# Sums and scales of four expert weights with priority, and their halves and the last transposes in another order, in a fused attention and mixture-of-experts kernel

## The chip, the cores and the metric

The kernel runs on one core of a Trainium2 chip. The metric is the device time of one launch in microseconds. The median of three runs of the kernel before is 670.71 us (669.89 to 672.58).

## The reference

Three layers follow one another over 1152 tokens with 512 features: attention that keeps the 32 largest scores of a row, a gated feed-forward layer behind an RMS norm, and a routed layer in which each token goes to one of eight experts.

```python
scores = scale * q @ k.T                                  # 2 x 8 heads, 576 x 576, head_dim 64
kth = 32nd largest of a row
attn = softmax(where(scores >= kth, scores, -1e9)) @ v
x = attn                                                  # 1152 x 512
xn = x / sqrt(mean(x * x) + 1e-6) * rms_g
x = (silu(xn @ w_gate) * (xn @ w_val)) @ w_out            # d_ff 1536
logits = x @ w_gate2                                      # 8 experts
e, p = argmax(logits), softmax(logits)[argmax]
out = p * (relu(x @ w1[e]) @ w2[e])                       # d_ff 1024; the first `capacity` = 288 tokens of an expert
```

## The kernel before, in words

The tokens are worked in nine tiles of 128 (NT = 9, tile 8 is the last). A hand-written order of slots (`at`, `advance`) sets when each part is traced: `topk`, `weights` and `values` (attention), `norm`, `moe1` (the gated layer) and `dispatch` (routing, and the scatter of a token's row into a table `disp` in DRAM, one region for each expert). Each part is a generator, and slots of several tiles interleave. What is traced gets a priority by its place in the program; `tc.high_priority(offset)` raises it. A list scheduler then fixes the order of every engine's queue from priorities and its own estimate of times; on the chip each queue runs in that order. `tc.issue_after(x)` keeps the instructions of a block that run on x's engine behind x in that queue; it does nothing to the other engines' instructions of the block. `after(t, name)` is such a tie to an instruction that was noted in `behind`.

Matrix products are done with numbers split into two fp16 halves, three matmuls for a product (high x high, high x low, low x high).

`norm` (L435) ends in four transposes into PSUM and `halves` (L469): ScalarE writes the high half of the transposed tile (L470), VectorE the low half (L471). `moe1` (L479) takes three groups of 512 hidden features; for each it makes a gate and a value product of 12 matmuls (L500), a tanh on ScalarE (L507), and two VectorE steps (L508, L511) that give the hidden tile h. `turned` (L483) transposes h in four matmuls (L486) and calls `halves` on the result, hT. The second product sums over 12 steps f of three matmuls (L525); steps 0 to 3 read hT of group 0, 4 to 7 that of group 1, 8 to 11 that of group 2. The result yx is copied by ScalarE (L531).

`dispatch` (L536) transposes yx (L540), multiplies by the router's matrix (L554), takes the logits (L557), makes the token's expert (L577 to L591), counts its place in the expert by two or three small matmuls (L593 to L595, L602), and gets the row number `slot` (L615). GpSimd then scatters the row (L617). For the last tile the gather of expert 0's first 128 rows (call k = "a", L612, issued by ScalarE's queue) starts as soon as the router's input is there; rows that the last tile adds to expert 0 are gathered later, by an indirect DMA of GpSimd (`rest_gather`, L890, k = "b") and a transposing DMA of SP's queue (L894).

The experts' weights w1 and w2 are 16 matrices of 2 MB, taken in the order 0, 1, 2, 3, 4, 6, 5, 8, 7 and so on (number 2e is w1 of expert e, 2e + 1 is w2). Each is loaded by SP's queue (L775). `size` (L780) squares it on ScalarE, in four pieces of 1024 columns for the first four weights (L791), casts the sums on VectorE (L794), adds them over the partitions by one matmul for each piece against ones (L796), and makes a power of two from the sum in five small VectorE steps (L797 to L802, with L148 and L151), one more for w2 (L806). `convert` (L809) makes the two halves: for the first four weights two pieces of the high half on ScalarE (L816), two on VectorE (L818), and four pieces of the low half on VectorE (L821). Weights 0 and 1 are loaded into the places that later hold the halves of weights 2 and 3, and the buffer of weight 2 takes weight 4 once weight 2's halves are made.

Around the change, `whole` traces these calls after the token tiles: `size(0)`, `size(1)`, `convert(0)`, `size(2)`, `convert(1)`, `convert(2)` with its VectorE part behind the last `halves` of tile 8, `size(3)`; then, behind the last router product on TensorE, the up product of expert 0's first 128 rows (`up("a")`, L907), `convert(3)` with its VectorE part behind the last `halves` of tile 8, the gathers for experts 1 to 3, and the loop over the experts, in which `ready` sizes and converts the later weights. `up` copies a product's relu as two halves (L917 on ScalarE, L918 on VectorE), `down` scales with VectorE (L926), `send` transposes back, scales and scatters the rows to the output (L985).

Of the kernel before, what the change touches and what calls it, by code (L numbers as in the profile page):

```python
# [1 line left out]

# [17 lines left out]
P = 128  # L20
# [42 lines left out]
def whole(  # L63
# [371 lines left out]
    def norm(t, ew):  # L435
        rs = mx.tile([P, H], F32, name="rs", bufs=2)
        (nc.gpsimd if t < NT - 1 else nc.vector).tensor_scalar(rs, sums[t], EPSD, None, op0=OP.add)
        yield
        nc.vector.reciprocal(rs, rs)
        u, v = ("xu", "x") if t < NT - 1 else ("x", "xu")  # L440
        xu = mx.tile([P, KC, P], F32, name=u)
        nc.scalar.activation(xu, xps.pop(t), AF.Copy)
        yield
        bank = "px" if t < NT - 1 else "xps"
        xt = px.tile([P, KC, P], F32, name=bank)
        for c in range(KC):
            nc.tensor.transpose(xt[:, c, :], xu[:, c, :], ident)
        x = mx.tile([P, DM], F32, name=v)
        nc.scalar.activation(x, xt.rearrange("p c j -> p (c j)"), AF.Copy)
        yield  # L450
        x3 = x.rearrange("p (h d) -> p h d", h=H)
        ew.tensor_tensor(x3, x3, rs[:, :, None].to_broadcast([P, H, D]), op=OP.mult)
        sq = mx.tile([P, DM], F32, name=u)
        ss = mx.tile([P, 2], F32, name="ss", bufs=2)
        nc.scalar.activation(sq, x, AF.Square, accum_out=ss[:, 0:1])
        yield
        nc.gpsimd.tensor_scalar(ss[:, 1:2], ss[:, 0:1], XS ** -2 / DM, XS ** -2 * 1e-6, op0=OP.mult, op1=OP.add)
        nc.gpsimd.tensor_tensor(ss[:, 0:1], ss[:, 1:2], mhalf, op=OP.pow)
        yield
        nc.scalar.activation(sq, x, AF.Copy, scale=ss[:, 0:1])  # L460
        yield
        xnT[t] = mx.tile([P, 2 * KC, P], F16, name="xn")
        xn = px.tile([P, KC, P], F32, name=bank)
        for c in range(KC):
            nc.tensor.transpose(xn[:, c, :], sq[:, c * P:(c + 1) * P], ident)
        halves(xnT[t], xn)
        yield

    def halves(out, x):  # L469
        nc.scalar.activation(out[:, :KC], x, AF.Copy)  # L470
        return nc.vector.tensor_tensor(out[:, KC:], x, out[:, :KC], op=OP.subtract)  # L471

    yx, late, behind = {}, [], {}

    def after(t, engine):

        return tc.issue_after(behind[t, engine].ins)

    def moe1(t, ew):  # L479
        hT = [mx.tile([P, 2 * KC, P], F16, name="hT", bufs=3) for _ in range(3)]  # L480
        xn = xnT.pop(t)

        def turned(g, h):  # L483
            tp = pm.tile([P, 4, P], F32, name="pm")
            for i in range(4):
                nc.tensor.transpose(tp[:, i, :], h[:, i * P:(i + 1) * P], ident)  # L486
            behind[t, "dve"] = halves(hT[g], tp)

        h = None
        for g in range(3):  # L490
            th = mx.tile([P, DM], F32, name="th")
            if ew is nc.gpsimd:
                gs = mx.tile([P, DM], F32, name="gs")
            for w in range(2):
                b = 2 * g + w
                a = late[0].tile([P, DM], F32, name="late") if late and b % 3 else pm.tile([P, DM], F32, name="pm")
                for c in range(KC):
                    i = KC * b + c
                    for n, (x, lo) in enumerate(((0, 0), (0, 1), (KC, 0))):
                        nc.tensor.matmul(a, xn[:, x + c, :], half(i, lo), start=(c == 0 and n == 0), stop=(c == KC - 1 and n == 2))  # L500
                    if c == 1:
                        yield
                    if c == 0 and w == 0 and h is not None:
                        turned(g - 1, h)
                yield
                if w == 0 and ew is nc.vector:
                    nc.scalar.activation(th, a, AF.Tanh, scale=gdec[:, g:g + 1])  # L507
                    nc.vector.scalar_tensor_tensor(th, th, 1.0, a, op0=OP.add, op1=OP.mult)  # L508
                elif ew is nc.vector:
                    h = mx.tile([P, DM], F32, name="x" if t == NT - 1 and g == 1 else "gs")  # L510
                    nc.vector.scalar_tensor_tensor(h, a, vg[:, g:g + 1], th, op0=OP.mult, op1=OP.mult)  # L511
                elif w == 0:
                    nc.scalar.activation(th, a, AF.Tanh, scale=gdec[:, g:g + 1])
                    nc.scalar.activation(gs, a, AF.Copy, scale=gdec[:, g:g + 1])
                    ew.tensor_tensor(th, th, gs, op=OP.mult)
                    ew.tensor_tensor(th, th, gs, op=OP.add)
                else:
                    h = mx.tile([P, DM], F32, name="gs")
                    nc.scalar.activation(h, a, AF.Copy, scale=vdec[:, g:g + 1])
                    ew.tensor_tensor(h, th, h, op=OP.mult)  # L520
        yps = pm.tile([P, DM], F32, name="pm")
        for f in range(NF1):
            i = final(6, f)
            for n, (hi, lo) in enumerate(((0, 0), (0, 1), (1, 0))):
                nc.tensor.matmul(yps, hT[f // KC][:, KC * hi + f % KC, :], half(i, lo), start=(f == 0 and n == 0), stop=(f == NF1 - 1 and n == 2))  # L525
            if f == 3:
                turned(2, h)
            if f % 2 == 1:
                yield
        yx[t] = route.tile([P, DM], F32, name="yx")  # L530
        nc.scalar.activation(yx[t], yps, AF.Copy, scale=ydec)  # L531
        yield
# [3 lines left out]
    def dispatch(t):  # L536
# [75 lines left out]
                gather("a", 0, 0, WA, ew, nc.scalar)  # L612
                notes("a", 0, 0, WA, ew, nc.scalar)
        slot = route.tile([P, 1], I32, name="slot")
        ev.tensor_scalar(slot, pos[:, 0:1], pos[:, 1:2], pos[:, 2:3], op0=OP.add, op1=OP.add)  # L615
        nc.gpsimd.tensor_tensor(cum, cum, oh, op=OP.add)
        scat.append(nc.gpsimd.indirect_dma_start(  # L617
            out=disp, out_offset=bass.IndirectOffsetOnAxis(ap=slot[:, :1], axis=0),
# [161 lines left out]
    def size(j, n):  # L780
# [5 lines left out]
        for g in range(k):  # L786
            if exact:
                junk = mx.tile([P, DM], F32, name="th").bitcast(BF16)
            else:
                junk = ew.tile([P, BIG], BF16, name="junk")[:, :2 * BIG // k]  # L790
            nc.scalar.activation(junk, raw[:, g * 2 * BIG // k:(g + 1) * 2 * BIG // k], AF.Square, accum_out=sc[:, 9 + g:10 + g])  # L791
        t = sums_of[:, n % 8:n % 8 + 1]
        s16 = ew.tile([P, 4], BF16, name="s16", bufs=2)
        nc.vector.tensor_copy(s16[:, :k], sc[:, 9:9 + k])  # L794
# [9 lines left out]
            es[e] = sc  # L804
        else:
            nc.vector.tensor_tensor(es[e][:, 8:9], es[e][:, 4:5], sc[:, 4:5], op=OP.mult)  # L806
        sized[j] = sc

    def convert(j, n):  # L809

# [53 lines left out]
    px.release()  # L864
    pm.release()
    wts.release()
    size(0, 0)
    size(1, 1)
    convert(0, 0)
    size(2, 2)  # L870
    convert(1, 1)
    with after(NT - 1, "dve"):
        convert(2, 2)
    fetch_w()
# [115 lines left out]

    with after(NT - 1, "pe"):
        up("a", 0, WA)
    with after(NT - 1, "dve"):
        convert(3, 3)
    last = gather(1, 1, 0, W, eb, nc.sync)
    rest_gather()
# [116 lines left out]
```

## Time and profile before

| | |
|---|---|
| median of 3 runs | 670.71 us |
| the profiled execution | 669.08 us |
| its span, first to last instruction | 667.2 us |
| mean granted TensorE clock | 0.975 |
| TensorE (PE) busy | 585.2 us, 88% |
| TensorE weight load (PEld) busy | 410.9 us, 62% |
| VectorE (DVE) busy | 535.9 us, 80% |
| ScalarE (ACT) busy | 500.5 us, 75% |
| GpSimd (POOL) busy | 353.6 us, 53% |
| chain that ended last | PE 54%, DVE 17%, DMA 9%, ACT 6%, POOL 6%, issue 5% |

Times in the rows are microseconds from the start of the span. An instruction's busy time on TensorE is modelled, since matmuls are pipelined. The attention ends near 454 us, the last tile's norm near 479, its gated layer at 517, its dispatch at 532, and the experts' products fill the rest. The granted clock is a share of 2.4 GHz: 1.00 is 2.4, 0.50 is 1.2.

### The profile page before, as it was taken

To read this page: it belongs to the slowest core of one execution; us is meant where nothing else is said; L and a number is where in the kernel's file an instruction comes from. 1 tells how busy PE (TensorE), PEld (TensorE's weight loads), DVE (VectorE), ACT (ScalarE), POOL (GpSimd) and SP (SyncE) were. 2 spreads that over 40 slices of the span, in tenths; PEclk is the share of its full clock that TensorE was granted. 3 is DMA by queue.
4 is the path that set the end of the run, shared out by engine and by line. 5 is a ranking of instruction groups with operands and counts; after the bars stand their busy time and mean duration, and the time that the engine had idled before them with its cause. 6 is when DMAs were issued, how large, how long until landed. Compare 5 with 4: busy or idle time off the path is not lost.

```text
span 667.2 us, 13474 instructions
## 1 busy us (share of the span) xinstructions
PE 585.2 (88%) x4817; PEld 410.9 (62%) x4817; DVE 535.9 (80%) x1495; ACT 500.5 (75%) x972; POOL 353.6 (53%) x490
## 2 busy tenths in 40 slices
PE   1427877899998999999999999999997569999994
PEld 1314454446665667666666666666553569999994
DVE  4989999978899878889889899762469646999961
ACT  4469978996788798887888787965975419999721
POOL 2487564445559699778689696782213000212112
PEclk9999979899999999999999999999998779999998
DMA  8998266923001010001000000008500489999001
GB/s 233 297 327 286 96 209 209 284 55 80 10 17 33 8 48 23 23 9 33 9 18 25 17 26 1 1 16 288 233 1 16 143 212 387 332 347 360 23 22 42
DMA packets 47006, 80.05 MB, mean 120 GB/s; under 512 B 18716, under 2 KB 23324, under 8 KB 46930
## 3 DMA queue, kind: packets, MB, share of 16 engines
q1 hardware_dynamic: 43938, 74.02, 34.8%
q0 software_dynamic: 1792, 4.83, 1.9%
q8 instruction: 39, 0.64, 0.4%
q10 hardware_dynamic: 1200, 0.26, 0.2%
q14 instruction: 37, 0.30, 0.2%
HBM read 64.35 MB, written 12.27 MB: 115 GB/s over the span
## 4 chain that ended last, share of the span: by engine, by line
PE 54%; DVE 17%; DMA 9%; ACT 6%; POOL 6%; issue 5%; SPq 1%; POOLq 0%; DVEq 0%; ACTq 0%
PE pm L500 17%; PE pm L525 9%; PE acc L907 8%; PE xps L430 6%; PE tp L317 5%; DVE split L821 5%; PE tp L422 4%; DMA vt<-in_v_l_dram 2%; DVE wbig L169 2%; DVE wbig L168 2%; DMA raw<-in_w_dram 2%; DVE r L373 2%; PE pm L486 2%; POOL pp L399 1%; DMA gk<-in_rms_g_dram 1%
## 5 line engine op out<-in xcount | busy, mean ns | idle before, releaser
L500 PE MATMUL pm<-wbig,xn 128*128 128x512 f16 x600 | 147.4, 379 | 0.1
L907 PEld LDWEIGHTS <-split 128*128 128x128 f16 x1728 | 116.8, 100 | 13.7 <-issue 6.6
L399 POOL TENSOR_TENSOR pp<-s,pp 128x576 f32<-128x576 f32 x72 | 101.9, 1431 | 16.6 <-ACT pp L398 16.3
L500 PEld LDWEIGHTS <-xn 128*128 128x128 f16 x648 | 62.3, 98 | 58.9 <-ACT xn L470 0.5
L376 DVE MAX8 m<-r 128x8 f32<-128x288 f32 x216 | 96.3, 453 | 2.4
L373 DVE MATCH_REPLACE8 r<-m,r 128x288 f32<-128x288 f32 x216 | 95.2, 443 | 0.0
L317 PE MATMUL tp<-kst,qh 128*128 128x288 f32 (+1 forms) x160 | 64.3, 410 | 32.3 <-ACT s L319 15.3
L525 PE MATMUL pm<-wbig,hT 128*128 128x512 f16 x324 | 79.5, 386 | 4.2 <-DVE hT L471 3.7
L319 ACT ACTIVATE s<-tp 128x288 f32<-128x288 f32 x144 | 57.3, 417 | 13.4 <-PE tp L317 11.1
L821 DVE SCALAR_TENSOR_TENSOR split<-raw,sc,split 128x2048 f16<-128x2048 f32 (+1 forms) x32 | 65.9, 2079 | 0.1
L907 PE MATMUL acc<-xgT,split 128*128 128x168 f16 (+1 forms) x768 | 58.0, 239 | 5.2 <-DMA xgT<-disp 5.2
L422 PE MATMUL tp<-ident,pp 128*128 128x128 f32 x324 | 57.5, 287 | 5.5 <-DVE r L325 2.4
L317 PEld LDWEIGHTS tp<-kst,qh 128*128 128x128 f32 (+1 forms) x160 | 31.2, 195 | 49.4 <-ACT s L319 21.1
L430 PE MATMUL xps<-pt,vt 128*64 128x128 f32 (+1 forms) x800 | 61.3, 273 | 0.0
L907 PE MATMUL acc<-hE,split 128*128 128x168 f16 (+2 forms) x864 | 58.9, 228 | 2.0 <-DVE sc L800 0.8
L398 ACT ACTIVATE pp<-s,bias 128x576 f32<-128x576 f32 x72 | 52.0, 775 | 10.0 <-POOL bias L381 10.0
L404 ACT ACTIVATE pp<-pp,bias 128x576 f32<-128x576 f32 x72 | 57.0, 794 | 3.1 <-POOL pp L399 3.0
L423 ACT ACTIVATE pt<-tp 128x384 f32<-128x384 f32 x108 | 52.0, 501 | 9.2 <-PE tp L422 7.0
L324 DVE TENSOR_TENSOR r<-tp,s 128x288 f32<-128x288 f32 x72 | 32.5, 451 | 29.0 <-ACT s L319 28.4
L422 PEld LDWEIGHTS tp<-ident,pp 128*128 128x128 f32 x324 | 40.2, 145 | 23.4 <-ACT pt L423 3.3
L791 ACT ACTIVATE junk<-raw 128x2048 bf16<-128x2048 f32 (+1 forms) x32 | 54.2, 1693 | 0.4
L525 PEld LDWEIGHTS <-hT 128*128 128x128 f16 x324 | 30.5, 99 | 37.8 <-DVE hT L471 4.2
(241 smaller groups left out, 1237.9 us busy)
## 6 DMA issues: line engine op xcount, KB each, us to landing
raw<-in_w_dram SPq DMA_DIRECT2D x28, 1024.0 KB, 9.3
wbig<-in_w_gate_dram SPq DMA_DIRECT2D x6, 1024.0 KB, 7.1
wbig<-in_w_val_dram SPq DMA_DIRECT2D x6, 1024.0 KB, 10.8
wraw<-in_w_out_dram SPq DMA_DIRECT2D x12, 512.0 KB, 6.3
disp<-wraw SPq DMA_DIRECT2D x18, 257.0 KB, 6.8
qraw<-in_q_l_dram SPq DMA_DIRECT2D x72, 64.0 KB, 2.3
wbig<-in_k_l_dram SPq DMA_DIRECT2D x16, 288.0 KB, 3.9
split<-in_w_dram SPq DMA_DIRECT2D x4, 1024.0 KB, 6.5
```

The source lines that it names most:

```text
L317: nc.tensor.matmul(sp[:c1], x[:, i, :c1], kst[b, hp][:, i, c * HALF:(c + 1) * HALF], start=(n == 0), stop=(n == 1))
L319: nc.scalar.activation(s[:, c * HALF:(c + 1) * HALF], sp, AF.Copy)
L373: nc.vector.match_replace(h[i], to[n - 1][:, i], h[i], -3.0e38)
L376: nc.vector.max(to[n][:, i], h[i])
L399: nc.gpsimd.tensor_tensor(w, s[i], w, op=OP.subtract)
L404: nc.scalar.activation(pp[p][:, i], pp[p][:, i], AF.Exp, bias=bias[:, i, 0:1], scale=0.125, accum_out=sums[t][:, h:h + 1])
L422: nc.tensor.transpose(tp[:, i, :], p2[:, o:o + P], ident)
L430: nc.tensor.matmul(xps[t][rows, hp, c0:c1], v, w, start=(n == 0), stop=(n == 4))
L500: nc.tensor.matmul(a, xn[:, x + c, :], half(i, lo), start=(c == 0 and n == 0), stop=(c == KC - 1 and n == 2))
L525: nc.tensor.matmul(yps, hT[f // KC][:, KC * hi + f % KC, :], half(i, lo), start=(f == 0 and n == 0), stop=(f == NF1 - 1 and n == 2))
L821: nc.vector.scalar_tensor_tensor(lo[:, r], raw[:, r], sc[:, 7:8], hi[:, r], op0=OP.mult, op1=OP.subtract)
L907: nc.tensor.matmul(a, u[:, c, col * P:(col + 1) * P], v[:, c, :a.shape[-1]], start=(c == 0 and n == 0), stop=(c == nk - 1 and n == 2))
```

## The change

It alters the order of some work and no arithmetic.

- The part of `size` behind the squares (cast, sum matmuls, scale) becomes a function `scale`. For the first four weights, in the part of the kernel that always runs, it is traced with a priority raised by 4000.
- The squares of weights 0 and 1 on ScalarE are tied behind the last norm's square (L455). VectorE's part of the halves of weights 0 and 1 is tied behind the last norm's low half (L471, tile 8).
- VectorE's part of the halves of weight 3 is tied behind the last `slot` (L615) in place of the last `halves`. That of weight 2 stays behind the last `halves`.
- In `moe1` the transposes of hidden group 2 are traced ahead of step 4's matmuls (before: behind step 3's, the same place), and for the last tile ahead of step 2's. For the last tile the matmuls of steps 0 and 1 are tied behind the last transpose of group 1, those of steps 2 to 11 behind the last transpose of group 2.

```diff
-        nc.scalar.activation(sq, x, AF.Square, accum_out=ss[:, 0:1])
+        behind[t, "sq"] = nc.scalar.activation(sq, x, AF.Square, accum_out=ss[:, 0:1])
...
-        halves(xnT[t], xn)
+        behind[t, "xn"] = halves(xnT[t], xn)
...
-    def after(t, engine):
+    def after(*what):
 
-        return tc.issue_after(behind[t, engine].ins)
+        return tc.issue_after(behind[what].ins)
...
             for i in range(4):
-                nc.tensor.transpose(tp[:, i, :], h[:, i * P:(i + 1) * P], ident)
+                behind[t, "turn", g] = nc.tensor.transpose(tp[:, i, :], h[:, i * P:(i + 1) * P], ident)
...
         for f in range(NF1):
             i = final(6, f)
-            for n, (hi, lo) in enumerate(((0, 0), (0, 1), (1, 0))):
-                nc.tensor.matmul(yps, hT[f // KC][:, KC * hi + f % KC, :], half(i, lo), start=(f == 0 and n == 0), stop=(f == NF1 - 1 and n == 2))
-            if f == 3:
+            if f == (2 if t == NT - 1 else 4):
                 turned(2, h)
+            with after(t, "turn", 1 if f < 2 else 2) if t == NT - 1 else nullcontext():
+                for n, (hi, lo) in enumerate(((0, 0), (0, 1), (1, 0))):
+                    nc.tensor.matmul(yps, hT[f // KC][:, KC * hi + f % KC, :], half(i, lo), start=(f == 0 and n == 0), stop=(f == NF1 - 1 and n == 2))
...
-        ev.tensor_scalar(slot, pos[:, 0:1], pos[:, 1:2], pos[:, 2:3], op0=OP.add, op1=OP.add)
+        behind[t, "slot"] = ev.tensor_scalar(slot, pos[:, 0:1], pos[:, 1:2], pos[:, 2:3], op0=OP.add, op1=OP.add)
...
+        with tc.high_priority(offset=4000) if n < 4 and not exact else nullcontext():
+            scale(e, w, n, k, sc)
+        sized[j] = sc
+
+    def scale(e, w, n, k, sc):
+
         t = sums_of[:, n % 8:n % 8 + 1]
...
-        sized[j] = sc
...
-    size(0, 0)
-    size(1, 1)
-    convert(0, 0)
+    with after(NT - 1, "sq"):
+        size(0, 0)
+        size(1, 1)
+    with after(NT - 1, "xn"):
+        convert(0, 0)
     size(2, 2)
-    convert(1, 1)
+    with after(NT - 1, "xn"):
+        convert(1, 1)
     with after(NT - 1, "dve"):
         convert(2, 2)
...
-    with after(NT - 1, "dve"):
+    with after(NT - 1, "slot"):
         convert(3, 3)
```

## Rows read from the trace of the kernel before

**Rows 1.** Waits from 440 us on: engine, line, releaser; total, times, longest.
```profile
PE acc L907 <- DMA xgT<-disp: 5.2, 1, 5.2
PE acc L907 <- DMA xbT<-xb: 4.8, 1, 4.8
PE pm L525 <- DVE hT L471: 3.7, 1, 3.7
...
PE acc L907 <- DVE sc L800: 0.8, 1, 0.8
...
PE acc L907 <- ACT junk L791: 0.2, 1, 0.2
```

**Rows 2.** Stretch, us; busy (xcount) of PE, PEld, DVE, ACT, POOL; clock, DMA share, GB/s.
```profile
480.00:490.00 10.00, 10.00 (x50) 4.79 (x49) 1.55 (x3) 9.81 (x19) 0.00 (x0) 1.00 0.00 0
490.00:510.00 20.00, 16.77 (x102) 9.18 (x100) 18.86 (x46) 11.19 (x19) 5.27 (x9) 1.00 0.00 1
510.50:517.20 6.70, 6.61 (x22) 2.46 (x22) 6.70 (x16) 4.27 (x4) 2.52 (x3) 0.75 0.10 39
543.50:548.00 4.50, 4.44 (x101) 4.44 (x102) 0.00 (x0) 0.38 (x1) 0.00 (x0) 0.50 0.98 292
560.00:640.00 80.00, 78.57 (x1073) 77.43 (x1071) 78.83 (x126) 68.77 (x75) 14.75 (x9) 1.00 0.79 258
```

**Rows 3.** TensorE in order of time: start, us, line, operation, idle before.
```profile
479.51 0.22 PE L796 MATMUL st<-s,ones 128*128 128x1 bf16 x3
...
491.03 0.17 PE L796 MATMUL st<-s,ones 128*128 128x1 bf16 x1
...
499.62 2.75 PE L500 MATMUL late<-wbig,xn 128*128 128x512 f16 x12
...
519.30 1.06 PE L554 MATMUL px<-rg,xu 128*128 128x8 f32 x8 [0.69 <-ACT xu L542]
525.52 3.99 PE L907 MATMUL acc<-xgT,split 128*128 128x128 f16 x43 [5.16 <-DMA xgT<-disp]
...
529.87 0.17 PE L594 MATMUL px<-oh,before 128*128 128x8 bf16 x1
```

**Rows 4.** VectorE in order of time.
```profile
478.08 0.69 DVE L471 TENSOR_TENSOR xn<-xps,xn 128x512 f16<-128x512 f32 x1 [0.64 <-ACT xn L470]
...
491.46 0.15 DVE L797 TENSOR_SCALAR sc<-st 128x1 f32<-128x1 f32 x1
...
504.11 0.74 DVE L511 SCALAR_TENSOR_TENSOR gs<-late,st,th 128x512 f32<-128x512 f32 x1
...
509.82 1.28 DVE L471 TENSOR_TENSOR hT<-pm,hT 128x512 f16<-128x512 f32 x2
...
521.48 2.47 DVE L821 SCALAR_TENSOR_TENSOR split<-raw,sc,split 128x1024 f16<-128x1024 f32 x2
...
523.93 0.15 DVE L557 COPY lg<-px 128x8 f32<-128x8 f32 x1
```

**Rows 5.** The squares of weights 0 and 1: ns min/median/max, first and last start.
```profile
L791 ACT ACTIVATE junk<-split x8: 1044/1050/1058, 468.0 to 479.1; 128x1024 bf16<-128x1024 f32 x8
```

**Rows 6.** VectorE by line, 474 to 532 us: the halves of weights 0 and 1.
```profile
L821 DVE SCALAR_TENSOR_TENSOR split<-split,sc,split 128x1024 f16<-128x1024 f32 x8 | 9.9, 1279 | 0.0
...
L818 DVE TENSOR_SCALAR split<-split,sc 128x1024 f16<-128x1024 f32 x4 | 2.8, 749 | 0.2 <-issue 0.2
```

**Rows 7.** Chain that ended last: ten second-product matmuls at full clock.
```profile
479.72 2.18 PE pm L525 x10
```

**Rows 8.** DMA issues, 440 to 560 us: count, median us to landing.
```profile
xgT<-disp SPq DMA_TRANSPOSE x4, 4.4
xgT<-disp ACTq DMA_TRANSPOSE x1, 6.8
```

**Rows 9.** GpSimd's instructions of two lines: ns min/median/max, first and last start.
```profile
L606 POOL TENSOR_SCALAR yd<-nm,yn x8: 268/268/1272, 202.4 to 508.6; 128x1 f32<-128x1 f32 x8
...
L617 POOL DMA_INDIRECT disp<-yd,slot x9: 1062/1123/1292, 208.0 to 532.3; - x9
```

More of the change, by code (lines that the diff above doesn't have):

```diff
@@ L1 @@
-from contextlib import ExitStack
+from contextlib import ExitStack, nullcontext
 import concourse.bass as bass
```

## The prediction

> **What bounds the kernel now.** I read the waits first, then TensorE's queue in order of time, then what VectorE did in the same microseconds, then busy time by stretch. TensorE is the busiest engine of the page, so I asked where it pauses in the last 230 us: three waits hold most of it, 5.2 us for a transposing gather, 4.8 us for the gather of expert 0's remainder, 3.7 us for the last halves of moe1's hidden tile [rows 1]. The reader is to see that the first of these is a DMA's own time, and that the other two end chains that run through VectorE.
>
> The stretches say why. From 480 to 490 us VectorE works 1.55 of 10 us, from 490 to 510 us 18.86 of 20, while TensorE is full in the first and misses 3.2 us in the second [rows 2]. TensorE's queue shows the cause: of the four sum matmuls of weight 0, three ran at 479.51 and the fourth at 491.03 [rows 3]; VectorE's first step on the sum follows at 491.46 [rows 4]. The squares were done long before: the eight of weights 0 and 1 began between 468.0 and 479.1 [rows 5]. So the halves of weights 0 and 1 fall into the 20 us in which the last two token tiles need VectorE. There the step that makes the last hidden tile, gs, starts at 504.11 although its matmuls, the twelve from 499.62 on, took 2.75 us and so ended near 502.4, and the halves of hT come only at 509.82, behind pieces of a split in VectorE's queue [rows 3, 4]. TensorE has nothing to do for 3.7 us before 510.5.
>
> **The pause in moe1.** The change gives the sums and scales of weights 0 to 3 priority 4000, and ties VectorE's part of the halves of weights 0 and 1 only behind the last norm, whose VectorE step runs at 478.08 [rows 4]. These halves are four tensor_scalar and eight scalar_tensor_tensor, 2.8 + 9.9 = 12.7 us [rows 6]. VectorE has 8.45 us free from 480 to 490, and from 490 on most of what it does is this very work [rows 2, 4], so it should be through near 495. Their cover is TensorE's own work on tiles 7 and 8, which is gapless there; if that cover failed, each piece (1.28 us) could stand ahead of a step that TensorE wants. With the queue clear, gs can start about 1.5 us earlier, and hT about 4 us earlier. The 3.7 us pause goes: **3.7 us**. The 22 matmuls behind it took 6.61 us at a mean granted clock of 0.75 [rows 2]; ten at full speed took 2.18 [rows 7], so 22 would take 4.8: **1.8 us**. A lower bound for this second term is 0 (the clock falls for another reason), the upper one is 1.8; I take 1.8 because TensorE then has no pause ahead of it.
>
> The transposes in fours: for the last tile the twelve-step sum now starts behind the four transposes of hidden group 1 and its third step waits for those of group 2. No instruction is added. Six matmuls (6 x 0.218 = 1.3 us) and the first four transposes stand between the end of gs's matmuls and the point where gs must be ready, while gs needs 0.74 [rows 4]. So 0 us, down to a loss of 0.74 if gs isn't hidden, and no gain beyond the pause already counted. For the other tiles the position of the transposes is the same as before, 0 us.
>
> The tie behind the last norm's square delays the first square, which began at 468.0 [rows 5], by up to 2 us. ScalarE is 98% busy from 480 to 490 but 56% in the next 20 us [rows 2], so it catches up: 0. What is late next is weight 2, whose halves still stand behind the last hT: 6.3 us of VectorE from about 506 to 512, under TensorE's last matmuls.
>
> **The dispatch of the last tile.** VectorE ran the last two pieces of weight 3's halves from 521.48 to about 523.9, and only then took the router's logits at 523.93, though TensorE's product for them had begun at 519.30 and ended near 520.4 [rows 3, 4]. Weight 3 now stands behind the slot, so 3.4 us of this wait go (523.93 less 520.4, less 0.1), on top of the 5.5 from moe1: the scatter starts 8.9 us earlier. The chain behind it (scatter, gather of the remainder, its transpose) is kept. TensorE itself arrives at the wait for the remainder 5.5 us earlier, so its 4.8 us pause shrinks by 3.4: **3.4 us**. It shrinks to zero if the sums for the slot also leave TensorE's queue earlier (they run at 529.87, behind 43 matmuls and more of the first up product, which began at 525.52 [rows 3]); that bound is 4.8. Behind the pause TensorE ran 4.5 us at clock 0.50 [rows 2]. With at most 1.4 us of pause left I take it that the clock stays up, as it stayed at 1.00 from 560 to 640 over a wait of 0.8 [rows 1, 2]; half of 4.5 is **2.2 us**. The lower bound is 0, if 1.4 is already too long.
>
> The gather that TensorE waits for first took 6.8 us to land, those on SP 4.4 in the median [rows 8]. It runs beside the load of weight 4, which starts when weight 2's halves have freed its buffer, and will run beside it again, so I take 0; the upper bound is 2.4, if the load is through earlier, and a loss is excluded, since the two collide already.
>
> Weight 3's halves themselves, 6.3 us of VectorE, move behind the slot, and what is queued behind them there is the first up product's relu halves and the halves of weight 4. Their cover is TensorE's first up and down product of expert 0, and weight 3 is first read in expert 1's second product, two products later; without the cover one piece, 1.28 us, is lost. From 560 to 640 us both engines are full, VectorE 78.83 and TensorE 78.57 of 80 [rows 2], so the gain survives only if both start earlier. SP's loads of the later weights stand in its queue behind the gathers that wait for the scatter, so they come forward with it.
>
> At the scatter the two engines meet. VectorE's work now begins right where GpSimd issues the indirect DMAs. The profile has both cases: an indirect DMA on GpSimd took 1062 to 1292 ns, and a one-column tensor_scalar, usually 268 ns, up to 1272, the last of eight at 508.6 among the splits [rows 9]. I take the indirect DMA's own spread, **0.2 us** lost. The Trainium skill, "SBUF — State Buffer", section "Who interferes with whom", says more: a VectorE instruction in a two-port mode holds the port pair it shares with GpSimd until it ends, and GpSimd blocks fully. By it the scatter and the remainder's gather would each wait a whole piece, 2 x 1.28, and the sum would be 8.5 us in place of 10.9. The spread of the indirect DMA's row does not show a whole piece.
>
> **Sum.** 3.7 + 1.8 + 3.4 + 2.2 - 0.2 = 10.9 us. The profiled execution took 669.08 us around a span of 667.2; it would take 658.2. The median of the three runs shown, 670.71, is 1.63 above it, so the forecast is **659.8 us**. With every bound at its good end the gain is 3.7 + 1.8 + 4.8 + 2.2 + 2.4 = 14.9, or 655.8.
>
> **Rivals.** *The dispatch stays gated by queue order.* TensorE's queue could keep the slot's sums behind those up matmuls, which wait for the gather. Gather and sums then both move only with moe1's end, and the 4.8 us pause and its slow clock stay: gain 5.5, 665.2 us; with moe1's clock term lost too, 667.0. For it: the order shown at 529.87. Against: in that order the logits had been held up by weight 3, which no longer stands there. Chance 0.20.
>
> *It doesn't do what it says.* ScalarE makes half of each weight's high halves and its queue holds 16 squares of 1.05 us [rows 5]; if its part comes only behind the squares of weights 2 and 3, the low halves still fall behind 490, and only weight 3's move counts: gain 3.4, 667.3 us, at the edge of what can be told. Against: what kept weight 0 back was the fourth sum matmul [rows 3], and that is what the priority moves. Chance 0.10.
>
> *TensorE waits at the heads of the sums: slower.* With priority the four groups of sum matmuls sit early in TensorE's queue, between 470 and 500 us, and each waits there for its last square. If the order was set for squares earlier than ScalarE delivers them, TensorE stands still. At 3.7 us, the length of the present pause, plus 1.8 for the clock, each group costs 5.5; two groups eat the gain, a third makes it slower, four give 22 - 11 = 11 us of loss, 682 us. For it: ScalarE is the fullest engine there beside TensorE [rows 2]. Against: TensorE waited 0.2 us in all for a square in the last 230 us [rows 1], and the three early sums show none [rows 3]. Chance 0.10.
>
> **How the numbers follow.** The forecast's case has 0.60; its bounds, 655.8 to 663.8 (both clock terms at 0), are its own range. It and the dispatch rival hold 0.80 together and reach from 655.8 to 667.0; 1 us more at the upper end is for the spread of the three runs (669.89 to 672.58). Rounded, 656 to 668. A measurement of this kernel tells about 0.5%, 3.4 us, from no change. Both of these cases gain more than that: faster 0.80. The rival in which only weight 3 moves is the same, 0.10. The waiting sums are slower, 0.10.
>
> **What would show it.** Right: the four sums of weight 0 together before 480 us; the split pieces of weights 0 and 1 between 479 and 497; no pause of TensorE between 500 and the end of moe1, which comes near 511; logits taken within 0.5 us of their product; scatter near 523; clock 1.00 where the remainder's product runs. The dispatch case: slot sums still behind dozens of up matmuls and a 4 to 5 us wait for the remainder. Wrong: waits of TensorE on ScalarE's squares or VectorE's casts between 470 and 500 us, split pieces of weight 1 still behind 500, or a stretch from 560 on that is longer than before by what was won.

## The result and the profile after

The changed kernel takes 676.64 us in the median of five runs (675.82 to 678.21), 1.0087 of the kernel before with a 95% interval of 1.0070 to 1.0104. It is slower by 0.9%, where 1.6% faster was forecast. The profiled execution has a span of 675.2 us (667.2 before) and a mean granted clock of 0.968 (0.975). The two profiled executions are 8.0 us apart, the two medians 5.9.

The line numbers have moved: L907 is now L916, L918 is L927, L926 is L935, L796 is L803, L821 is L827, L615 is L616, L617 is L618. The waits of TensorE from 440 us on, with the columns of [rows 1]:

```profile
PE acc L916 <- DMA xbT<-xb: 4.4, 1, 4.4
PE acc L916 <- DVE sc L806: 4.0, 1, 4.0
PE late L500 <- DVE gs L511: 3.3, 1, 3.3
PE acc L916 <- DVE hE L927: 2.1, 1, 2.1
PE px L595 <- DVE pos L600: 1.6, 1, 1.6
PE acc L916 <- DMA xgT<-disp: 1.6, 1, 1.6
PE pm L486 <- DVE gs L511: 1.3, 1, 1.3
```

The 3.7 us wait for hT of [rows 1] is gone, and the first gather is waited for 1.6 us in place of 5.2. The wait for the remainder has shrunk by only 0.4, and five waits are new or longer: 3.3 and 1.3 us on gs, 2.1 us on relu halves, 1.6 us on a step of the slot (pos), and 4.0 us on "sc L806", a scale. The stretches, with the columns of [rows 2]:

```profile
480.00:490.00 10.00, 10.00 (x57) 4.96 (x56) 6.05 (x14) 9.84 (x18) 1.03 (x2) 1.00 0.07 26
490.00:500.00 10.00, 6.68 (x35) 3.36 (x34) 9.82 (x19) 10.00 (x19) 1.12 (x2) 0.92 0.01 2
...
600.00:640.00 40.00, 35.20 (x456) 34.60 (x454) 38.19 (x58) 28.30 (x32) 7.82 (x6) 0.96 0.41 135
```

VectorE does work earlier, as meant: 6.05 us in place of 1.55 from 480 to 490. But it is full from 490 to 500, and there TensorE misses 3.3 us. From 600 to 640 TensorE misses 4.8 us, where the kernel before missed 0.4 (39.58 of 40). TensorE in order of time:

```profile
484.32 0.24 PE L803 MATMUL st<-s,ones 128*128 128x1 bf16 x4
...
498.24 1.28 PE L500 MATMUL late<-wbig,xn 128*128 128x512 f16 x3 [3.32 <-DVE gs L511]
...
538.58 1.06 PE L916 MATMUL acc<-xbT,split 128*128 128x48 f16 x22 [4.40 <-DMA xbT<-xb]
539.47 6.38 PE L916 MATMUL acc<-hE,split 128*128 128x128 f16 x83
...
559.68 3.51 PE L916 MATMUL acc<-xgT,split 128*128 128x168 f16 x25 [2.06 <-DVE hE L927]
...
633.69 8.77 PE L916 MATMUL acc<-hE,split 128*128 128x168 f16 x96 [4.03 <-DVE sc L806]
642.29 7.12 PE L916 MATMUL acc<-xgT,split 128*128 128x168 f16 x96
```

The four sums of weight 0 do run together, but at 484.32, where "before 480" was asked for. VectorE in the same microseconds:

```profile
480.51 0.30 DVE L801 CAST s<-sc 128x4 bf16<-128x4 f32 x1 [0.34 <-ACT junk L792]
...
494.99 2.47 DVE L827 SCALAR_TENSOR_TENSOR split<-split,sc,split 128x1024 f16<-128x1024 f32 x2
...
497.45 0.74 DVE L511 SCALAR_TENSOR_TENSOR gs<-late,st,th 128x512 f32<-128x512 f32 x1
...
498.17 2.47 DVE L827 SCALAR_TENSOR_TENSOR split<-split,sc,split 128x1024 f16<-128x1024 f32 x2
...
525.37 0.27 DVE L616 TENSOR_SCALAR slot<-pos 128x1 int32<-128x1 f32 x1
...
628.44 4.60 DVE L827 SCALAR_TENSOR_TENSOR split<-raw,sc,split 128x2048 f16<-128x2048 f32 x2
632.97 0.67 DVE L927 SCALAR_TENSOR_TENSOR hE<-acc,hE 128x504 f16<-128x504 f32 x1
```

Read the two fences together. At 497.45 gs comes from behind two pieces of weight 1, and TensorE resumes at 498.24, as soon as gs ends. At 632.97 the relu halves of expert 6's first product come from behind 4.60 us of pieces. Expert 5's second product needs a PSUM buffer that they free, by the code; it starts at 633.69 and then runs 8.77 us, at a mean granted clock of 0.80, where the same 96 matmuls take 7.12 at 1.00. (The profile names the scale L806 as the releaser; it lies between the relu halves in VectorE's queue.)

| | before | after |
|---|---|---|
| end of moe1 of the last tile (yx) | 517.21 | 519.38 |
| slot of the last tile | 531.17 | 525.37 |
| its scatter on GpSimd | 532.31 | 527.48 |
| first product of expert 0 starts | 525.52 | 526.51 |
| count matmul behind the remainder's second product | 558.06 | 557.43 |
| first product of expert 7 starts | 634.21 | 642.29 |

So the dispatch did come 5 to 6 us earlier, and near 557 the new kernel led by 0.6 us. The loss of 8 us lies behind that: 2.06 us and a slow clock (0.84 from 560 to 570) at 559.68, and 4.03 plus 1.65 us at 633.69.

### The profile page after: what moved, and what is told of

Same layout as the page of the kernel before. It is cut to its first block, busy times and chain, and to the rows that moved or that the text cites. A ratio compares the mean times of both kernels' runs of the same rounds, so it can differ in the third digit from the quotient of the medians.

```text
span 675.2 us, 13473 instructions
## 1 busy us (share of the span) xinstructions
PE 590.7 (87%) x4817; PEld 415.1 (61%) x4817; DVE 542.5 (80%) x1495; ACT 502.8 (74%) x972; POOL 346.4 (51%) x490
## 5 line engine op out<-in xcount | busy, mean ns | idle before, releaser
L916 PEld LDWEIGHTS <-split 128*128 128x128 f16 x1728 | 119.7, 101 | 14.0 <-issue 8.2
L528 PE MATMUL pm<-wbig,hT 128*128 128x512 f16 x324 | 76.7, 380 | 0.0
L916 PE MATMUL acc<-hE,split 128*128 128x168 f16 (+2 forms) x864 | 62.4, 235 | 4.8 <-DVE sc L806 4.0
L827 DVE SCALAR_TENSOR_TENSOR split<-raw,sc,split 128x2048 f16<-128x2048 f32 (+1 forms) x32 | 65.6, 2077 | 0.4 <-ACT split L822 0.4
L916 PE MATMUL acc<-xgT,split 128*128 128x168 f16 (+1 forms) x768 | 58.8, 240 | 3.7 <-DVE hE L927 2.1
L430 PEld LDWEIGHTS xps<-pt,vt 128*64 128x64 f32 x800 | 43.9, 138 | 13.7 <-issue 12.0
```

The lines of the kernel that those rows point to most:

```text
L430: nc.tensor.matmul(xps[t][rows, hp, c0:c1], v, w, start=(n == 0), stop=(n == 4))
L827: nc.vector.scalar_tensor_tensor(lo[:, r], raw[:, r], sc[:, 7:8], hi[:, r], op0=OP.mult, op1=OP.subtract)
L916: nc.tensor.matmul(a, u[:, c, col * P:(col + 1) * P], v[:, c, :a.shape[-1]], start=(c == 0 and n == 0), stop=(c == nk - 1 and n == 2))
```

## The experiments

Theory Q: the order of VectorE's queue decides, split pieces against the short steps that TensorE waits for, and the moved transposes change that order everywhere. Its first rivals: H, the early halves of weights 0 and 1 cost what they give; S, weight 3's move is a plain gain. The order of the queues, read from the traces, bears on Q. The kernel after leaves the order of the kernel before in the first token tile, at 174 us, on TensorE and on VectorE; the run without the transposes edit leaves it only at 473 us on TensorE and at 470 on VectorE, where the ties begin; the run with weight 3 alone moved, which has the new functions too, at 524 and 519. Profiles with one and the same order start up to 5 us apart (the first tile's yx comes at 183.97 before, at 189.24 in the run with weights 0 and 1 alone), so times are compared between profiles that agree there to about 1 us, or as differences within a profile.

**The parts one by one.** The change without its transposes edit:

```diff
-            if f == (2 if t == NT - 1 else 4):
-                turned(2, h)
-            with after(t, "turn", 1 if f < 2 else 2) if t == NT - 1 else nullcontext():
-                for n, (hi, lo) in enumerate(((0, 0), (0, 1), (1, 0))):
-                    nc.tensor.matmul(yps, ...)
+            for n, (hi, lo) in enumerate(((0, 0), (0, 1), (1, 0))):
+                nc.tensor.matmul(yps, ...)
+            if f == 3:
+                turned(2, h)
             if f % 2 == 1:
                 yield
```

> The change without its edit of the transposes (step order and ties of the second product as before, on all nine tiles). Theory Q (what decides is where VectorE's queue puts split pieces against the steps TensorE waits for, and the moved transposes changed that order everywhere): 660 to 666 us; gated layer of the last tile ends by 515, wait for the remainder at most 2 us, in the last experts the relu halves come before the split pieces and TensorE waits under 1 us. Rival H (the early halves of weights 0 and 1 cost what they give, whatever the transposes do): 672 to 678 us, with a wait of TensorE for gs or th of 3 us or more near 495.

662.19 us, 0.9883 (0.9833 to 0.9933): Q. The time lies in the range that was forecast for the whole; the gain is 8.3 us, where 10.9 was forecast. TensorE's queue, in order of time, shows both terms of the prediction:

```profile
507.04 5.66 PE L525 MATMUL pm<-wbig,hT 128*128 128x512 f16 x24 [0.22 <-ACT hT L470]
...
521.05 1.44 PE L915 MATMUL acc<-xgT,split 128*128 128x128 f16 x12 [4.73 <-DMA xgT<-disp]
522.28 0.21 PE L594 MATMUL px<-oh,before 128*128 128x8 bf16 x1
...
530.19 5.46 PE L915 MATMUL acc<-hE,split 128*128 128x128 f16 x95 [0.40 <-DVE hE L926]
536.13 2.60 PE L915 MATMUL acc<-xbT,split 128*128 128x48 f16 x96 [0.48 <-DMA xbT<-xb]
```

The pause before the second product of moe1 is 0.22 us, and the pause for the remainder 0.48. Look at the order: all of expert 0's second product stands ahead of the remainder's first product here. In the kernel after, 22 matmuls of the remainder stand ahead of 83 of that product. The slot's sums do stand behind 12 up matmuls here, which wait 4.73 us for the gather, as the prediction's dispatch rival had it; the wait for the remainder went all the same. Expert 1's first product starts 8.8 us earlier than before (538.57 against 547.41), expert 2's 6.1 (552.02 against 558.11): in between TensorE waits 0.9 us on relu halves and 1.8 on the casts of a sum. The rest of the lead is kept, 6.0 us at expert 7's first product (628.25).

The kernel before with only the transposes edit:

```diff
-            for n, (hi, lo) in enumerate(((0, 0), (0, 1), (1, 0))):
-                nc.tensor.matmul(yps, ...)
-            if f == 3:
+            if f == (2 if t == NT - 1 else 4):
                 turned(2, h)
+            with after(t, "turn", 1 if f < 2 else 2) if t == NT - 1 else nullcontext():
+                for n, (hi, lo) in enumerate(((0, 0), (0, 1), (1, 0))):
+                    nc.tensor.matmul(yps, ...)
```

> The kernel before with the edit of the transposes alone. Theory Q: 670 to 676 us, the last norm 2 to 4 us later than before, halves of weights 0 and 1 still behind 490. Rival H: 669 to 672, no difference that can be told.

677.92 us, 1.0129 (1.0073 to 1.0184): slower, and 1.9 us more than Q's range. GpSimd's queue, in order of time, shows where:

```profile
519.30 2.39 POOL L616 TENSOR_SCALAR slot<-pos 128x1 int32<-128x1 f32 x1
521.97 1.78 POOL L618 DMA_INDIRECT disp<-yd,slot  x1 [0.29 <-POOL slot L616]
530.27 0.18 POOL L546 COPY yd<-tok 128x1 f32<-128x1 f32 x1 [6.51 <-DMA disp<-yd,slot]
```

Split pieces filled VectorE from 513.8 to 526.3. Beside them the slot of the last tile but one took 2.39 us and its scatter 1.78 (0.38 and 1.12 in the kernel after), and the scatter landed only at 530.27; the gather behind it kept TensorE waiting 11.2 us. The landing took 6.51 us (1.96 in the kernel after). A weight's load was issued at 520.31, too, and no run shows how much of the 6.51 is the load's and how much the pieces'.

Only weights 0 and 1, then only weight 3:

```diff
+        with tc.high_priority(offset=4000) if n < 4 and not exact else nullcontext():
+            scale(e, w, n, k, sc)
...
+    with after(NT - 1, "sq"):
         size(0, 0)
         size(1, 1)
+    with after(NT - 1, "xn"):
         convert(0, 0)
     size(2, 2)
+    with after(NT - 1, "xn"):
         convert(1, 1)
```

> The kernel before with the priority of the sums and scales and the ties of weights 0 and 1 alone; weight 3 and the transposes as before. Theory Q: 663 to 668 us: the pause of 3.7 us in the gated layer goes or halves, the logits are still taken behind weight 3's pieces, the 4.8 us wait for the remainder stays. Rival H: 673 to 678 us.

666.88 us, 0.9945 (0.9918 to 0.9973): Q again, H falls.

```diff
-    with after(NT - 1, "dve"):
+    with after(NT - 1, "slot"):
         convert(3, 3)
```

> The kernel before with weight 3's halves behind the last slot alone. The logits are taken at once and the slot comes 4 to 6 us earlier under both. Theory Q: the loss turns up later, since the order of the relu halves and the split pieces in the last experts is that of the changed kernel: TensorE waits 3 to 5 us near 625 to 635, 669 to 675 us. Rival S (the move of weight 3 is a plain gain): 664 to 667 us, no such wait.

682.29 us, 1.0177 (1.0123 to 1.0231): S falls, and the loss is larger than Q's. The tail has the 4.0 us wait that Q expected. Another part is at the scatter, on GpSimd, and behind it on VectorE, each in order of time:

```profile
529.89 4.01 POOL L617 DMA_INDIRECT disp<-yd,slot  x1 [4.50 <-DMA notes<-disp]
536.10 0.97 POOL L895 DMA_INDIRECT xb<-disp,rest  x1 [2.19 <-DMA disp<-yd,slot]
```

```profile
528.11 4.87 DVE L826 SCALAR_TENSOR_TENSOR split<-raw,sc,split 128x1024 f16<-128x1024 f32 x4
...
541.06 0.15 DVE L939 CAST to<-xb 48x1 int32<-48x1 f32 x1 [6.52 <-DMA xb<-disp,rest]
...
541.89 0.68 DVE L923 SCALAR_TENSOR_TENSOR hE<-acc,hE 128x512 f16<-128x512 f32 x1
```

The scatter first waits for the notes gather that reads the same table, then takes 4.01 us beside four pieces (1.06 to 1.29 in [rows 9]), ending 0.9 us behind the last of them. The late gather holds up a cast on VectorE, and the relu halves stand behind that cast.

The parts don't add up: alone they give -0.55% and +1.77%, together (the first run) -1.17%.

**The tail.** The change, with the fifteenth weight's conversion traced one product later and tied:

```diff
+            behind["hE", k] = nc.vector.scalar_tensor_tensor(hl, a, 0.0, hh, op0=OP.max, op1=OP.subtract)
...
         if done[0] < 2 * E - 1:
-            ready()
+            with after("hE", 6) if e == 6 else nullcontext():
+                ready()
...
         down(e - 1, e - 1, W)
-        ready()
+        if e != 5:
+            ready()
```

> The whole change, with one thing more at the end: the halves of the fifteenth weight on VectorE are tied behind the relu halves of expert 6's first product, so that these no longer stand behind 4.6 us of pieces. Theory Q (the order of VectorE's queue decides): down of expert 5 gets its buffer without the 4.0 us wait on the scale L806, and runs at 7.1 instead of 8.8 us, so 676.6 - 4.0 - 1.65 = 671, range 669 to 674. Rival W (the last weights come late whatever stands ahead of them, so the wait only moves): the wait comes back in front of expert 7's first product, 675 to 678.

670.08 us, 0.9994 (0.9966 to 1.0022), Q's range. Against the change's 1.0087 that is 0.93%, some 6.2 us, where 5.7 was expected. TensorE there:

```profile
630.24 1.98 PE L916 MATMUL acc<-hE,split 128*128 128x168 f16 x25
632.11 5.31 PE L916 MATMUL acc<-hE,split 128*128 128x168 f16 x71
637.25 7.12 PE L916 MATMUL acc<-xgT,split 128*128 128x168 f16 x96
```

Expert 7's first product starts at 637.25 in place of 642.29, and its 96 predecessors took 7.2 us in place of 8.77. Up to 621 us TensorE's and VectorE's queues have the order of the kernel after, and no pause comes back ahead of expert 7: rival W falls.

**The two halves of the transposes edit.** First the last tile's form alone, then tiles 0 to 7 alone, each with the rest of the change:

```diff
-            if f == (2 if t == NT - 1 else 4):
+            if f == 2 and t == NT - 1:
                 turned(2, h)
...
+            if f == 3 and t < NT - 1:
+                turned(2, h)
             if f % 2 == 1:
                 yield
```

> The whole change, but the transposes of hidden group 2 in tiles 0 to 7 are issued where the kernel before has them, in front of the yield; only the last tile has the new form. Theory Q, with the loss put down to the move in tiles 0 to 7, which shifts the order of both queues from the first tile on: near the run without the transposes edit (662.2), 660 to 666, moe1's end near 513 us. Rival L (the last tile's new form itself costs, its sum waits for the transposes of group 1 and 2): 670 to 678, with a wait of TensorE on gs or hT between 500 and 515 as in the change.

```diff
-            if f == (2 if t == NT - 1 else 4):
+            if f == 4 and t < NT - 1:
                 turned(2, h)
-            with after(t, "turn", 1 if f < 2 else 2) if t == NT - 1 else nullcontext():
-                for n, (hi, lo) in enumerate(((0, 0), (0, 1), (1, 0))):
-                    nc.tensor.matmul(yps, ...)
+            for n, (hi, lo) in enumerate(((0, 0), (0, 1), (1, 0))):
+                nc.tensor.matmul(yps, ...)
+            if f == 3 and t == NT - 1:
+                turned(2, h)
```

> The whole change, but the last tile has its old form; only tiles 0 to 7 issue the transposes of hidden group 2 behind the yield. Theory Q with the loss in tiles 0 to 7: the last norm's square again near 473, moe1's end near 518 to 520; the tail has another order (the relu halves of expert 6 ahead of the fifteenth weight's pieces), so up to 5.7 us better than the change: 670 to 677. Rival L (the last tile's form costs): 660 to 666.

667.9 us (0.9968, 0.9941 to 0.9996) and 672.1 us (1.0020, 0.9985 to 1.0054; ten runs from 667.4 to 675.86, of which the fastest was profiled). The second is in Q's range, the first between both theories' ranges: the last tile's form costs, too. The first has the order of the run without the edit up to 502 us, the second that of the kernel after up to 509. The end of moe1 separates the halves of the edit cleanly: 512.74 without the edit, 511.74 with the last tile's form alone, 518.32 with tiles 0 to 7 alone, 519.38 with both. Tiles 0 to 7 cost moe1 5.6 to 7.6 us; the last tile's form moves its end by 1 us, once forward and once back, no more than the profiles' starts differ. What the last tile's form does cost comes behind moe1; VectorE and GpSimd of that run:

```profile
516.80 0.27 DVE L618 TENSOR_SCALAR slot<-pos 128x1 int32<-128x1 f32 x1
...
521.06 3.67 DVE L829 SCALAR_TENSOR_TENSOR split<-raw,sc,split 128x1024 f16<-128x1024 f32 x3
524.65 0.16 DVE L606 RECIPROCAL nm<-nm 128x1 f32<-128x1 f32 x1
524.72 0.73 DVE L573 SCALAR_TENSOR_TENSOR yd<-yx,yn,yd 128x512 f16<-128x512 f32 x1
```

```profile
527.77 1.06 POOL L620 DMA_INDIRECT disp<-yd,slot  x1 [8.56 <-ACT hE L928]
```

The slot is there at 516.80, 6.2 us earlier than in the run without the edit (523.03), but the scatter 3.6 us later (524.16 there). It also needs the scaled row and its weight, and those stand behind weight 3's pieces, which are tied behind the slot alone. TensorE then waits 4.6 us for the remainder, 0.5 in the run without the edit.

**The scatter.** The kernel before with weight 3 alone moved, still further:

```diff
+            behind["hE", k] = nc.vector.scalar_tensor_tensor(hl, a, 0.0, hh, op0=OP.max, op1=OP.subtract)
...
-    with after(NT - 1, "dve"):
+    with after("hE", "a"):
         convert(3, 3)
```

> The kernel before with only weight 3 moved, but further: behind the relu halves of the first product instead of behind the slot, so that no split piece runs on VectorE while GpSimd issues the scatter. Theory P (the pieces hold GpSimd up, and the scatter took 4.0 us because of them): the scatter takes 1.0 to 1.5 us, the gather behind it comes 2.5 to 3 us earlier, and the time falls from 682.3 to 676 to 680. Rival D (the scatter took 4.0 us for the DMA that it waited for, or for its own work): it takes 3.5 to 4.5 us again, and the time stays within 680 to 684.

677.33 us, 1.0107 (1.0074 to 1.0140), theory P: rival D falls. GpSimd, beside the fence of the run with weight 3 behind the slot:

```profile
529.53 1.06 POOL L617 DMA_INDIRECT disp<-yd,slot  x1 [4.24 <-DVE to L939]
533.05 0.97 POOL L895 DMA_INDIRECT xb<-disp,rest  x1 [2.47 <-DMA disp<-yd,slot]
```

With no piece beside it the scatter takes 1.06 us, and the gather comes 3.05 us earlier. The 4.0 us wait of the tail isn't in this run, and TensorE waits 6.7 us on relu halves where the other waited 2.2, so the 5 us between the two are not the scatter's alone.

**Repairs.** The run with the last tile's form alone, weight 3 tied behind all that the scatter reads; then the casts of the gathered notes tied behind the relu halves as well; then the casts' tie on the whole change:

```diff
+            behind[t, "row"] = nc.vector.scalar_tensor_tensor(yl, y, yn[:, 5:6], yh, op0=OP.mult, op1=OP.subtract)
...
+        behind[t, "weight"] = ev.tensor_scalar(yd[:, DM:DM + 1], nm[:, 3:4], yn[:, 2:3], 1.0 / YS, op0=OP.mult, op1=OP.mult)
...
-    with after(NT - 1, "slot"):
+    with after(NT - 1, "slot"), after(NT - 1, "row"), after(NT - 1, "weight"):
         convert(3, 3)
```

> The run with the last tile's new form alone (667.9), and weight 3 tied behind all three steps that the scatter reads, the slot, the scaled row and its weight, instead of the slot alone. Theory Q (in that run the slot was there at 516.8, but the row and its weight stood behind the pieces of weight 3 and the scatter came at 527.8): the scatter comes near 522 and the 4.6 us wait for the remainder's transpose shrinks below 1; but four casts that read gathered notes now stand ahead of the first relu halves and hold them until about 531, so 2 to 4 us of a wait on the relu halves come instead: 662 to 668. Rival D (the scatter waits for the landing of the gather that reads the same table): the scatter stays behind 525 and the wait for the remainder stays above 3 us.

669.15 us, 0.9981 (0.9955 to 1.0007). The scatter left 10.9 us behind the transposes of the last yx on TensorE (525.39 less 514.47), in the run before 15.3 (527.77 less 512.48): the tie gave 4.4 us. The scatter still came behind 525, as D had it (this profile starts 1.9 us later than that of the run before), but the wait for the remainder fell from 4.6 us to 0.2, and so D falls. As expected the casts then held TensorE:

```profile
PE acc L918 <- DVE hE L929: 4.5, 3, 2.0
PE acc L918 <- DVE to L975: 3.2, 1, 3.2
```

It waited 3.2 us on a cast and 4.5 us, in three waits, on relu halves. The sum, 1.2 us above Q's range, is no gain.

```diff
-            nc.vector.tensor_copy(to[:m], meta[k, i][:m, 1:2])
+            with after("hE", "a") if k == "b" else nullcontext():
+                nc.vector.tensor_copy(to[:m], meta[k, i][:m, 1:2])
...
+            with after("hE", "a"):
                 nc.vector.tensor_copy(targets[i][:m, 1:], every[i][:m, 1:, 1])
...
+            with after("hE", "a"):
                 nc.vector.tensor_copy(to[:m], every[i][:m, k, 1:2])
```

> The run before, and the casts of the gathered notes tied behind the second relu halves of expert 0's first product. Theory Q: both waits go, 667.9 - 4.6 = 663.3, and up to 2 more for the clock behind them: 659 to 664. Rival D: as in the run before, 666 to 669.

> The whole change with one thing more: the casts of the gathered notes tied behind the second relu halves of expert 0's first product. Theory Q (in the change these halves stood behind casts that waited for a DMA until 536): the second halves run near 534, down a does not stand behind the 22 matmuls of the remainder, the 4.4 us wait for the remainder's transpose falls on a later matmul or shrinks: 676.6 - 3 to 5 = 671.5 to 674. Rival (TensorE would wait for the remainder anyway): 675.5 to 677.5.

669.16 us (0.9981, 0.9959 to 1.0003) and 675.83 us (1.0061, 1.0032 to 1.0090). Both miss Q's range; the second lies in its rival's. VectorE and TensorE of the second say why:

```profile
537.53 0.69 DVE L927 SCALAR_TENSOR_TENSOR hE<-acc,hE 128x512 f16<-128x512 f32 x1
```

```profile
542.07 1.06 PE L916 MATMUL acc<-xbT,split 128*128 128x48 f16 x22 [4.30 <-DMA xbT<-xb]
542.96 6.59 PE L916 MATMUL acc<-hE,split 128*128 128x128 f16 x83
```

The relu halves no longer stand behind the casts and end near 538.2, but TensorE's own queue still has 22 matmuls of the remainder ahead of 83 that need only expert 0. It waits for the remainder wherever the casts are (4.04 us in the first of the two). The rival was right here: not VectorE's queue alone decides, TensorE's does too. No run gives the changed kernel's TensorE the other order by itself.

The change without the transposes edit a second time; its edit is that of the first run:

> The change without its transposes edit, a second time, on the same chip as the three above, to rank it with them. It took 662.2, 0.9883 of the kernel before; by theory Q it lies again between 0.983 and 0.993, and within 3 us of the version with the row's tie and the casts behind the relu halves.

662.28 us, 0.9867 (0.9840 to 0.9894). It beats the kernel before, the change, and every repair; the version with both ties lies 6.9 us behind it, not 3.

## Why the prediction was wrong

**The step that failed** is the price of the transposes, and above all one sentence: "For the other tiles the position of the transposes is the same as before, 0 us." It isn't the same, nor is it "the same place" that the description of the change has. Behind step 3 stands a yield, so a transpose ahead of step 4 is traced one slot of the interleaving later, behind other generators' work. Every queue has another order from the first tile on. TensorE there, and the last norm's square on ScalarE, each before and after:

```profile
173.57 1.67 PE L525 MATMUL pm<-wbig,hT 128*128 128x512 f16 x7
174.29 0.60 PE L486 MATMUL pm<-ident,gs 128*128 128x128 f32 x4
...
469.33 0.62 ACT L455 ACTIVATE x<-xu 128x512 f32<-128x512 f32 x1
473.46 0.63 ACT L455 ACTIVATE x<-xu 128x512 f32<-128x512 f32 x1 [0.20 <-DVE xu L452]
```

The tiles' ends move both ways: tile 4's yx comes 2.3 us earlier (372.02 to 369.73), tile 6's 6.0 us later (456.24 to 462.23). The last norm's square comes 4 us later, the first square of weight 0, tied behind it, at 474.08 instead of 470.07 in the run without the edit, and the four sums at 484.32 instead of 479.17. Weights 0 and 1 are halved 5 us later than in that run, and so in front of gs.

The last tile's form was put at 0 us, "down to a loss of 0.74 if gs isn't hidden". In the kernel after its transposes wait 1.27 us for gs. Alone it holds the scatter back, with a wait of 4.6 us for the remainder; since the repairs of that gained nothing, how much of its price this is stays open. By the ratios (0.9883 without the edit, 0.9968, 1.0020, 1.0087) the last tile's form alone costs some 6 us, tiles 0 to 7 some 9, both 14.

The rest, by the prediction's own steps:

- **Early halves, 3.7 + 1.8 us.** Right in the main without the transposes edit: moe1 ended 4.5 us earlier (512.74; 5.5 forecast), with the clock at 1.00 from 507 to its end. With the edit the moe1 pause moved from hT to gs, 3.3 us, and moe1 ended 2.2 us later. "... if that cover failed, each piece (1.28 us) could stand ahead of a step that TensorE wants" named this danger, and no rival priced it. The rival with waits at the heads of the sums did not happen: no wait on a square is among the longest.
- **Dispatch, 3.4 + 2.2 us.** The logits no longer wait behind pieces (522.62, after 0.80 us idle for their product), and the slot's sums run at 524.67, ahead of expert 0's first product: the dispatch rival is not the case. But the scatter moved by 4.8 us, not 8.9. In the two runs with weight 3 alone moved it waited for the notes gather that reads its table, a floor that the prediction didn't see. In the kernel after, the pause stayed at 4.4 us for two reasons: the relu halves stood behind casts until 537.8, and TensorE's queue put the 22 matmuls of the remainder ahead. Without the transposes edit it was 0.48.
- **The scatter beside VectorE, 0.2 us.** Mis-sized: 4.01 us against 1.06 in the pair of runs on weight 3, so 3.0. The kernel after lost 0.5 (1.61 us). The rule that the prediction weighed, from the Trainium skill, "SBUF — State Buffer", section "Who interferes with whom", is that GpSimd blocks fully while a VectorE instruction in a two-port mode has the shared ports. Both losses agree with it in kind, though no run shows in which mode the pieces ran; 0.5 us is less than the one piece (1.28) that the prediction put on it, 3.0 us is more.
- **Weight 3's pieces, "without the cover one piece, 1.28 us, is lost".** Wrong in kind. Moved alone they cost 1.8%. That run and the kernel after both have the 4.03 us wait of the tail, 100 us on: the order of later conversions against relu halves has moved with them. Without the transposes edit, with weight 3 moved all the same, the wait isn't there, so the tail hangs on the edits together.
- **560 to 640, "the gain survives only if both start earlier".** TensorE reached the count matmul 0.6 us earlier, and still 8 us were lost, because the order inside the full queue had changed. Without the transposes edit the lead of 6 us at expert 2 was still there at expert 7. The run that ties one weight's pieces behind one product's relu halves gives back 6.2 us of it.

For the change without its transposes edit, 662.2 us, the range of 656 to 668 holds and so does the way the waits fell; the sum was 2.6 us too high, about what TensorE waits between the first products of experts 1 and 2 there, which the sum hadn't priced.

## What to carry to other kernels

Where a list scheduler orders the queues, "moved over a yield" is no small edit: compare the whole order of each queue before and after, ahead of any sum of waits, and price each long instruction that has come to stand ahead of a short one on which the fullest engine waits. A tie behind one operand protects that operand alone; tie behind all that the next step reads. And each part of a change that only reorders has to be measured by taking it out of the whole: parts that alone gained 0.55% and lost 1.77% gained 1.17% together. Why they do so isn't shown here beyond the order of the queues.

## What the runs showed of the hardware

Beside four pieces in a row on VectorE, GpSimd's indirect DMA took 4.01 us, and 1.06 with the pieces moved away. Beside such pieces it took 1.61 us in the kernel after, where it began with the first of two pieces under way:

```profile
526.88 2.47 DVE L827 SCALAR_TENSOR_TENSOR split<-raw,sc,split 128x1024 f16<-128x1024 f32 x2
...
527.48 1.61 POOL L618 DMA_INDIRECT disp<-yd,slot  x1 [2.33 <-DVE split L824]
```

The first piece ends near 528.1 by half of the 2.47 us, the scatter 1.0 us later. In three other runs (1.78, 1.78 and 2.05 us) it also ends about 1.0 us behind the end of the piece in which it began; in the run with 4.01 us it began in the second of four pieces and ended 0.9 us behind the fourth. Why it was held so long isn't shown. A one-column tensor_scalar of GpSimd took 2.39 us beside pieces (0.38 for the same step in the kernel after). The price of a pause on TensorE differs for the same wait: behind 4.03 us on the same scale, 96 matmuls took 8.77 us in the kernel after and 9.57 in the run with the casts tied, against 7.12 at a granted clock of 1.00, so 1.65 and 2.45 us more.
